# Handing out PSUM banks and softmax buffers by release, and a new order of the first part, in a recurrence and feed-forward kernel on one core

## The chip, the core and the metric

The kernel runs on one core of a Trainium2 chip. A core has five engines with queues of their own: TensorE (PE, matrix products, with its weight loads as PEld), VectorE (DVE), ScalarE (ACT), GpSimd (POOL) and SyncE (SP, which here starts nearly all DMAs). Matrix products land in PSUM, which has eight banks of 128 x 512 float32. The metric is the device time of one execution in microseconds (us), as the median of several runs; lower is better.

## The reference, cut to what matters

```python
batch, H, S, D, N, chunk = 4, 8, 768, 32, 16, 32
log_a = np.log(np.clip(a, 1e-06, 1.0))
for c in range(S // chunk):
    cum = np.cumsum(la, axis=-1)                        # la, xc, Bc, Cc: this chunk's
    L = np.exp(cum[:, :, :, None] - cum[:, :, None, :]) * causal
    M = np.einsum('bhin,bhjn->bhij', Cc, Bc) * L
    y_intra = np.einsum('bhij,bhjd->bhid', M, xc)
    y_inter = np.einsum('bhin,bhnd->bhid', Cc, state) * np.exp(cum)[:, :, :, None]
    y[:, :, sl] = y_intra + y_inter
    Bx = np.einsum('bhjn,bhjd->bhjnd', Bc, xc) * np.exp(cum[:, :, -1:] - cum)[..., None, None]
    state = np.exp(np.sum(la, axis=-1))[:, :, None, None] * state + np.sum(Bx, axis=2)
x = y as (3072 tokens, 256)
h = x @ w_in                                            # w_in: 256 x 2048
g = np.maximum(h, 0.0) + np.log1p(np.exp(-np.abs(h)))   # softplus
return g @ w_out                                        # w_out: 2048 x 256
```

## The kernel before

The 768 positions are cut into six rounds u of 128 positions. One round holds the four batches, 512 tokens in all, in two pairs of batches p. A round of the recurrence is made of these steps; the word in brackets is the one by which the order names it. Decay factors are exponentials of sums of logarithms, by token (`ft`) and by row (`fr`). POOL lays them out as a 128 x 512 triangle for each head pair (D, the affine selects that write `rm`). PE makes scores (S, four banks `sp` at a time, 32 short matmuls) and DVE multiplies them into the triangles (M, `rm<-sp,rm`). PE makes values within the round (I, `yp`), the new state (U, `zp`; N on DVE writes it as `tb`) and what the old state adds (R, also into `yp`, from C scaled by DVE, `cc`). DVE multiplies by the growth (G, `gg`). Then the result is split for the feed-forward part into a high part on ACT and a low part on DVE (Xh, Xl).

The feed-forward part of a round has 16 blocks k. Each is three products in split precision, high by high, low by high and high by low, of two halves of the contraction: six matmuls of 512 columns into a bank `hp` (F). ACT takes the softplus (`e<-hp`) and the high part `gh`, DVE the low part `gl<-e,gh` (P, in three stages). Six more matmuls add the block to the output sums in the two `acc` banks (Z): for each half of the output `gh` by the high weights, `gl` by the high weights, `gh` by the low weights `wol`, in this order. The weights themselves arrive as 64-bit numbers and are split on the way: three ACT steps, one DVE step that joins bits (`w<-w,signs`), the high part on ACT and the low part on DVE (`wil`, `wol`; the stages of W).

What sets the order. The whole first part is written out by hand as a string of words, `ORDER` (line 62); `act` looks each word up in the table `acts` and calls the step. Up to step 42 of the feed-forward part (`PINNED`) every instruction is kept in program order on its engine. Afterwards a scheduler orders the rounds 3 to 5, whose steps the table `FILLS` puts at given distances. All helpers record their operations in line 140, so rows of the profile carry L140 for most of the kernel, and are told apart by the names of the tiles.

What the change touches. `ps` (line 128) is a pool of six PSUM banks that are given out in rotation: the seventh tile takes the bank of the first, whoever has emptied its bank by then. Every `ps.tile` of log sums, factors, scores, `zp`, `yp` and `hp` comes from it. The softmax sums `e` rotate in the same way through three buffers of the pool `p3` (`parts_of`). `first_logs` (line 153) holds the logarithms of rounds 0 and 5 and a third group for the growth of round 0; `other_logs` holds the rest. `factors_by_token` makes fp (four products) and total (one), which PE works off in two passes each, and `factors_by_row` makes `sums` and `rp`; group 0 of each uses the first logs where it can. `warm` issues matmuls of 512 columns on a tile of zeros, `zeros<-some`, that nothing reads.

```python
ps = ctx.enter_context(tc.tile_pool(name="ps", bufs=6, space=PSUM))
pa = ctx.enter_context(tc.tile_pool(name="pa", bufs=1, space=PSUM))
e = p3.tile([P, 512], F32, tag="e", name=f"e{j}_{k}")
```

Of the kernel before, what the change touches and what calls it, by code (L numbers as in the profile page):

```python
# [41 lines left out]
ROW_GROUPS = ((1, LAST), (LAST, NU))  # L42
# [11 lines left out]
C_MID = C_OWN + (LAST - 1) * NB * (NC + 1)  # L54
# [6 lines left out]
la warm6 warm1 warm1 warm1 loga lb logb loga kb gc fr1 logr gb ft0 logr fr1 us0.0 ft0 ft0 w0 ft0 gc ft0 S0.0 growth  # L61
growth ft0 ux0.0 logb D0.0.0 D0.0.2 us0.1 M0.0.0 D0.0.1 M0.0.2 D0.0.3 W0 W0 M0.0.1 gq D0.1.0 ft1 ux0.1 M0.0.3 gq B0.0
W0 W0 fr0 I0.0 fr1 B0.1 gq gq ft1 D1.0.3 gq S0.1 G0.0 w2 Xh0.0 W2 W2 fr0 M0.1.0 W0 ft1 un1.0 W2 growth D0.1.1 M0.1.1
w1 fr0 D0.1.2 D0.1.3 fr0 M0.1.2 w4 ft1 fr1 D1.0.0 tl un1.1 M0.1.3 U0 W0 Xl0.0 I0.1 G0.1 Xh0.1 W2 W2 un2.0 N0 D1.1.0
S1.0 W4 Xl0.1 H0 W4 D1.0.2 M1.0.0 H1 W2 F0.1 M1.0.3 w6 W4 w3 P0.1 F0.0 D1.1.2 D1.1.3 T1 D1.0.1 F0.2 M1.0.2 D1.1.1 W4
P0.0 gd M1.0.1 W1 B1.1 S1.1 F0.3 W1 W4 M1.1.0 W1 W4 P0.2 w7 W1 w5 P0.0 M1.1.1 B1.0 W1 W1 F0.4 P0.0 P0.1 W6 P0.1 P0.2
M1.1.3 P0.3 P0.3 M1.1.2 W3 W3 W3 gg1 F0.5 Z0.0 C1 Z0.1 P0.2 W3 P0.4 W6 U1 N1 P0.3 I1.0 P0.5 W6 W6 W3 W3 I1.1 W6 D2.1.1
S2.0 P0.5 W7 R1 Z0.2 G1.0 D2.0.3 G1.1 Xh1.0 W7 P0.4 D2.0.2 D2.0.0 D2.0.1 W6 w10 Z0.3 M2.0.3 W7 F0.6 P0.6 Xh1.1 Xl1.0
W5 F0.7 Xl1.1 W7 P0.5 F1.5 M2.0.1 w12 W5 W7 W5 F1.0 P0.7 P0.7 P0.4 P0.6 W5 w14 P0.7 W5 W5 M2.0.0 F1.2 W12 M2.0.2 W12
D2.1.0 W12 F1.3 Z0.4 P1.3 B2.0 Z0.5 w9 P0.6 w8 W12 P1.0 W12 F1.6 W7 P1.2 W10 P1.3 W10 P1.3 P1.2 F1.1 P1.2 Z0.6 P1.1  # L70
Z0.7 K0.1 W10 P1.1 K0.0 W10 w11 P1.0 W12 P1.6 W10 P1.0 W10 F1.4 W9 F1.7 F0.12 P1.1 P1.4 Z1.0 P1.6 W9 P1.5 W8 W8 Z1.1
F1.12 W8 W8 un3.1 P1.6 Z1.2 D2.1.2 W9 P1.5 W8 F0.13 F1.10 P1.7 W9 W9 W8 Z1.3 F0.9 P1.5 W14 P0.12 W9 P1.4 P1.4 Z1.4
P0.9 W11 Z1.5 W14 W14 P0.12 W11 T2 W14 W11 W11 F0.8 Z1.6 w15 P1.7 P1.7 F0.10 P0.8 Z1.7 W11 gg3 P0.8 F0.11 W14 W11 W14
un3.0 P0.8 W15 K1.1 D2.1.3 F0.15 K1.0 w13 W13 Z0.8 W15 P0.10 P0.10 P0.9 F1.8 P0.12 P0.10 gg2 P0.13 P0.11 W13 W13 P0.9
W13 Z0.9 Z0.10 P0.15 P0.15 P0.11 P0.11 F0.14 P0.14 Z0.11 F1.11 P0.13 W13 un2.1 P0.14 P0.13 W13 P0.14 P0.15 Z0.12 Z0.13
W15 F1.9 W15 W15 P1.8 P1.8 P1.10 P1.11 W15 Z0.14 Z0.15 P1.8 D3.0.3 E0 P1.9 F1.14 Z1.8 B2.1 P1.9 P1.10 P1.9 C2 D3.0.2
P1.10 S2.1 M2.1.3 P1.12 M2.1.2 Z1.9 I2.0 P1.12 M2.1.0 M2.1.1 U2 I2.1 N2 P1.14 P1.14 P1.12 R2 P1.14 G2.0 S3.0 M3.0.2
D3.0.1 G2.1 P1.11 Xh2.0 Xl2.0 F1.15 Z1.10 M3.0.1 Xh2.1 P1.11 P1.15 P1.15 F1.13 D3.0.0 M3.0.3 Z1.11 P1.15 P1.13 M3.0.0
Xl2.1 P1.13 P1.13
"""  # L80
HALF = NFT // 2
# [14 lines left out]
    (-5, "U@ I@.0 I@.1 R@ S@+.0 G@.0 G@.1 N@ Xh@.0 Xh@.1 Xl@.0 Xl@.1"),  # L96
# [3 lines left out]
def constants():  # L100
# [7 lines left out]
    unit = np.arange((LAST - 1) * NB * (NC + 1)) // (NC + 1)  # L108
# [11 lines left out]
def recurrence_then_ffn(ctx: ExitStack, tc: tile.TileContext, un, alr, w_in, w_out, const, outT):  # L120
# [32 lines left out]
    first_logs = cp.tile([P, 3 * NR], F32, name="first_logs")  # L153
    other_logs = cp.tile([P, NA - 2 * NR + NL], F32, name="other_logs")
    lo, lr = other_logs[:, : NA - 2 * NR], other_logs[:, NA - 2 * NR :]
# [66 lines left out]
    def sum_logs():  # L222
        gp = ps.tile([P, 512], F32, tag="ps", name="log_sums")[:, :P]
        for b in range(NB):
            PE.matmul(
                gp[NR * b : NR * b + NR].rearrange("p (c k) -> p c k", k=SUB),
                first_logs[:, 2 * NR :],
                kc[:, : NC * (P + SUB)].rearrange("p (c k) -> p c k", k=P + SUB)[:, :, :SUB],
                start=True,
                stop=True,  # L230
            )
        yield
        by_head_row[0] = p3.tile([P, 2 * RT], F32, tag="xh", name="by_head_row")[:, :P]
        V.tensor_copy(by_head_row[0], gp)

    def growth_on_chip():
        gg_s[0] = p2.tile([P, 2, RT], F32, tag="gg", name="gg0")
        gp = [
            early_bank(b % 2, f"gp{b}") if b < 2 else ps.tile([P, 512], F32, tag="ps", name=f"gp{b}")
# [12 lines left out]
        for b in range(NB):  # L252
# [6 lines left out]
            )  # L259

# [32 lines left out]
    zeros = []  # L293

    def warm(n):
        if not zeros:
            zeros.append(ps.tile([P, 512], F32, tag="ps", name="zeros"))
        for _ in range(n):
# [6 lines left out]
            )  # L305

# [5 lines left out]
    cp.tile([P, 56], F32, name="apart")  # L312
    for u in range(NU):
        ks = slice(u * NR, (u + 1) * NR)
        f_tok[u] = ft[:, ks], fc[:, ks]
        f_row[u] = fr[:, u * NB : (u + 1) * NB]

    def factors_by_token(g):
        us = (0, LAST) if g == 0 else range(1, LAST)
        logs = first_logs[:, : 2 * NR] if g == 0 else lo  # L320
        n = len(us) * NR
        fp = ps.tile([P, 512], F32, tag="ps", name=f"fp{g}")
# [4 lines left out]
        runs = ((0, 1), (LAST, NU)) if g == 0 else ((1, LAST),)  # L327
        total, at = None, 0
        for u0, u1 in runs:
            here, cols = slice(at, at + (u1 - u0) * NR), slice(u0 * NR, u1 * NR)  # L330
            at = here.stop
            A.activation(fc[:, cols].rearrange("p k c -> p c k"), by_chunk[:, :, here], AF.Exp)
            yield
            if total is None:
                total = ps.tile([P, 512], F32, tag="ps", name=f"total{g}")[:, :n]
                PE.matmul(total, kc[:, NC * P : K_END], logs, start=True, stop=True)
                yield
            A.activation(ft[:, cols], total[:, here], AF.Exp)
            yield

    def factors_by_row(g):
        u0, u1 = ROW_GROUPS[g]
        logs = lo if g == 0 else first_logs[:, NR : 2 * NR]
        n, nu = (u1 - u0) * NR, (u1 - u0) * NB
        sums = ps.tile([P, 512], F32, tag="ps", name=f"sums{g}")[:n, : NC + 1]
        PE.matmul(sums, logs, kb[:, C_MID:C_HEAD], start=True, stop=True)
        yield
        by_head = p2.tile([P, (LAST - 1) * NB, NC + 1], F32, tag="by_head", name=f"by_head{g}", bufs=1)[:n, :nu]
# [5 lines left out]
        )  # L354
        yield
        rp = ps.tile([P, 512], F32, tag="ps", name=f"rp{g}")
# [95 lines left out]
    def update(u):  # L452
        zp = mid[u]["zp"] = ps.tile([P, 512], F32, tag="ps", name=f"zp{u}")
# [435 lines left out]
```

## Time and profile before

| what | before |
|---|---|
| median of 3 runs | 314.68 us (314.35 to 315.39) |
| profiled execution | 314.79 us, span 313.1 us |
| PE busy | 306.8 us, 98% of the span, 2325 matmul records |
| DVE busy | 155.8 us, 50% |
| ACT busy | 168.1 us, 54% |
| POOL busy | 43.6 us, 14% |
| DMA | 24.38 MB |

The times in this table and in the rows below are of one profiled execution, apart from the median. A row of the timeline is a run of like instructions on one engine: where it starts, how long it lasts, the operation with the tile written and the tiles read, shapes and count, and in brackets the idle time in front of it with what ended that. An instruction that has begun and is held up inside counts as busy, so starts of rows that follow one another are read along with the busy time.

### The profile page before, as it was taken

To read this page: it belongs to the slowest core of one execution; us is meant where nothing else is said; L and a number is where in the kernel's file an instruction comes from. 1 tells how busy PE (TensorE), PEld (TensorE's weight loads), DVE (VectorE), ACT (ScalarE), POOL (GpSimd) and SP (SyncE) were. 2 spreads that over 40 slices of the span, in tenths; PEclk is the share of its full clock that TensorE was granted. 3 is DMA by queue.
4 is the path that set the end of the run, shared out by engine and by line. 5 is a ranking of instruction groups with operands and counts; after the bars stand their busy time and mean duration, and the time that the engine had idled before them with its cause. 6 is when DMAs were issued, how large, how long until landed. Compare 5 with 4: busy or idle time off the path is not lost.

```text
span 313.1 us, 5688 instructions
## 1 busy us (share of the span) xinstructions
PE 306.8 (98%) x2325; PEld 251.8 (80%) x2325; DVE 155.8 (50%) x262; ACT 168.1 (54%) x292; POOL 43.6 (14%) x59
## 2 busy tenths in 40 slices
PE   8899999999999999999999999999999999999995
PEld 5778888888888788888888888888888888888884
DVE  5899866464566954453932352642352332322222
ACT  3898978778947244344344534344534344634450
POOL 2880710003130720100300000300000000000000
PEclk9999999999999999999999999999999999999999
DMA  7995442466201440100610100000100000100001
GB/s 214 404 386 163 137 134 69 167 176 214 81 0 67 137 137 4 66 0 0 228 45 0 67 2 0 4 0 0 67 4 0 2 0 2 67 0 0 2 0 67
DMA packets 10442, 24.38 MB, mean 78 GB/s; under 512 B 1200, under 2 KB 1840, under 8 KB 10416
## 3 DMA queue, kind: packets, MB, share of 16 engines
q1 hardware_dynamic: 10416, 24.02, 22.4%
q8 instruction: 18, 0.29, 0.4%
q14 instruction: 8, 0.07, 0.1%
HBM read 20.77 MB, written 3.24 MB: 77 GB/s over the span
## 4 chain that ended last, share of the span: by engine, by line
PE 95%; DVE 3%; ACT 1%; issue 0%; POOL 0%; POOLq 0%
PE acc L140 41%; PE hp L140 41%; PE yp L140 5%; PE sp L140 4%; DVE rm L140 1%; PE zeros L140 1%; PE end L140 1%; PE fp L140 1%; PE zp L140 1%; DVE xl L140 0%; DVE w L140 0%; DVE wil L140 0%; DVE gg L140 0%; ACT fc L140 0%; ACT signs L140 0%; PE rp L140 0%
## 5 line engine op out<-in xcount | busy, mean ns | idle before, releaser
L654 DVE TENSOR_TENSOR gl<-e,gh 128x512 fp32r<-128x512 f32 x54 | 37.3, 692 | 92.0 <-ACT gh L651 92.0
L140 PE MATMUL hp<-xh,wih 128*128 128x512 f32 (+1 forms) x196 | 75.8, 387 | 0.4 <-DVE gg L140 0.4
L140 PE MATMUL hp<-xh,wil 128*128 128x512 f32 (+1 forms) x196 | 75.4, 385 | 0.0
L140 PE MATMUL hp<-xl,wih 128*128 128x512 f32 (+1 forms) x196 | 75.4, 385 | 0.0
L140 PE MATMUL acc<-gh,woh 128*128 128x512 f32 x188 | 74.1, 394 | 0.0
L648 ACT ACTIVATE e<-hp 128x512 f32<-128x512 f32 x54 | 32.3, 598 | 77.7 <-PE hp L140 77.4
L140 PE MATMUL acc<-gl,woh 128*128 128x512 f32 x188 | 73.3, 390 | 0.0
L140 PE MATMUL acc<-gh,wol 128*128 128x512 f32 x188 | 73.2, 389 | 0.0
L140 PEld LDWEIGHTS hp<-xh,wih 128*128 128x128 f32 x196 | 36.8, 188 | 8.2 <-DVE gg L140 0.6
L140 DVE TENSOR_TENSOR gl<-e,gh 128x512 fp32r<-128x512 f32 x42 | 31.1, 749 | 24.3 <-ACT gh L140 24.2
L140 PEld LDWEIGHTS hp<-xl,wih 128*128 128x128 f32 x196 | 36.8, 188 | 7.3
L140 PEld LDWEIGHTS hp<-xh,wil 128*128 128x128 f32 x196 | 36.8, 188 | 7.3
L140 POOL TENSOR_SCALAR_AFFINE_SELECT rm<-fc 128x512 f32<-128x512 f32 x36 | 32.5, 939 | 70.2 <-ACT signs L140 41.9
L140 PEld LDWEIGHTS acc<-gh,woh 128*128 128x128 f32 x188 | 35.3, 188 | 8.2 <-ACT gh L140 0.2
L140 PEld LDWEIGHTS acc<-gh,wol 128*128 128x128 f32 x188 | 35.3, 188 | 7.4
L140 PEld LDWEIGHTS acc<-gl,woh 128*128 128x128 f32 x188 | 35.3, 188 | 7.3 <-DVE gl L654 0.2
L140 ACT ACTIVATE e<-hp 128x512 f32<-128x512 f32 x42 | 24.3, 592 | 23.8 <-PE hp L140 20.7
L651 ACT CAST gh<-e 128x512 fp32r<-128x512 f32 x54 | 33.5, 621 | 4.1 <-PE acc L140 2.4
L140 ACT CAST gh<-e 128x512 fp32r<-128x512 f32 x42 | 25.4, 616 | 5.3 <-PE acc L140 4.8
L140 ACT ACTIVATE signs<-wraw 128x512 f16<-128x512 f32 (+1 forms) x32 | 23.9, 781 | 0.0
L140 DVE TENSOR_TENSOR rm<-sp,rm 128x512 f32<-128x512 f32 x32 | 20.8, 682 | 3.7 <-PE sp L140 3.7
L404 POOL TENSOR_SCALAR_AFFINE_SELECT rm<-fc 128x512 f32<-128x512 f32 x12 | 9.1, 792 | 87.1 <-PE yp L140 69.4
(106 smaller groups left out, 212.3 us busy)
## 6 DMA issues: line engine op xcount, KB each, us to landing
un<-in_un SPq DMA_DIRECT2D x10, 768.0 KB, 6.4
wraw<-in_w_in SPq DMA_DIRECT2D x8, 512.0 KB, 5.0
wraw<-in_w_out SPq DMA_DIRECT2D x8, 512.0 KB, 3.8
gg<-gd SPq DMA_DIRECT2D x20, 128.0 KB, 3.9
out_t<-o SPq DMA_DIRECT2D x9, 256.0 KB, 2.1
head_in_h<-in_un SPq DMA_DIRECT2D x2, 384.0 KB, 5.2
head_in_l<-in_un SPq DMA_DIRECT2D x2, 384.0 KB, 6.9
out_t<-half SPq DMA_DIRECT2D x2, 256.0 KB, 2.1
```

What stands on the lines that cost most here:

```text
L140: return lambda *a, **k: tc.keep_in_program_order(f(*a, **k))
L404: Pl.affine_select(out=weights_of(u, p, ks.start, ks.stop).rearrange("p h (c i) -> p (h c) i", i=SUB), in_=fs.rearrange("p h c -> p (h c)" ...
L648: A.activation(e, h, AF.Softplus)
L651: A.copy(gh, e)
L654: V.tensor_tensor(gl, e, gh.bitcast(F32), op=ALU.subtract)
```

## The change

Four edits go together. The six banks become six tiles of one buffer each, and a list of free banks is kept while the program is written: `take` hands out the bank that came back first, and `done` is called right after the last step that reads it, so the next tile takes the bank which is emptied first in the order of the program. The three softmax buffers are handled in the same way. The first logs hold rounds 0, 1, 2 and 5 instead of 0 and 5 (160 columns instead of 96; the other logs 256 instead of 320 ahead of the growth), and the columns of all factors follow this order of rounds. `ORDER` is a new string, in which the nine warm matmuls are six, one, one and one. In `FILLS` one word, N, stands earlier in its row.

```diff
-ROW_GROUPS = ((1, LAST), (LAST, NU))
+SLOTS = (0, 1, 2, LAST, 3, 4)
+NS = 4
...
 ORDER = """
-la warm6 warm1 warm1 warm1 loga lb logb loga kb gc fr1 logr gb ft0 logr fr1 us0.0 ft0 ft0 w0 ft0 gc ft0 S0.0 growth
...
+warm6 la loga loga lb logr logr growth ft0 logb ft0 kb ft0 warm1 us0.0 gc ft0 growth D0.0.0 ft0 ft0 D0.1.3 D0.0.1 gb
...
-    (-5, "U@ I@.0 I@.1 R@ S@+.0 G@.0 G@.1 N@ Xh@.0 Xh@.1 Xl@.0 Xl@.1"),
+    (-5, "U@ I@.0 I@.1 R@ N@ S@+.0 G@.0 G@.1 Xh@.0 Xh@.1 Xl@.0 Xl@.1"),
...
-    ps = ctx.enter_context(tc.tile_pool(name="ps", bufs=6, space=PSUM))
+    ps = ctx.enter_context(tc.tile_pool(name="ps", bufs=1, space=PSUM))
...
+    class Ring:
+        def __init__(self, pool, tag, n, dtype):
+            self.pool, self.tag, self.dtype = pool, tag, dtype
+            self.free, self.held = deque(range(n)), {}
+        def take(self, name):
+            k = self.held[name] = self.free.popleft()
+            return self.pool.tile([P, 512], self.dtype, tag=f"{self.tag}{k}", name=name, bufs=1)
+        def done(self, name):
+            self.free.append(self.held.pop(name))
+    banks = Ring(ps, "ps", 6, F32)
+    soft = Ring(p3, "e", 3, F32)
...
-    first_logs = cp.tile([P, 3 * NR], F32, name="first_logs")
-    other_logs = cp.tile([P, NA - 2 * NR + NL], F32, name="other_logs")
+    first_logs = cp.tile([P, (NS + 1) * NR], F32, name="first_logs")
+    other_logs = cp.tile([P, NA - NS * NR + NL], F32, name="other_logs")
...
-            mid[u]["sp", p, q] = ps.tile([P, 512], F32, tag="ps", name=f"sp{u}_{p}{q}")
+            mid[u]["sp", p, q] = banks.take(f"sp{u}_{p}{q}")
...
         V.tensor_tensor(m, mid[u].pop(("sp", p, q)), m, op=ALU.mult)
+        banks.done(f"sp{u}_{p}{q}")
...
-        e = p3.tile([P, 512], F32, tag="e", name=f"e{j}_{k}")
+        e = soft.take(f"e{j}_{k}")
         A.activation(e, h, AF.Softplus)
+        banks.done(f"hp{j}_{k}")
...
         V.tensor_tensor(gl, e, gh.bitcast(F32), op=ALU.subtract)
+        soft.done(f"e{j}_{k}")
```

The order on the engines at three places. The first is PE in the opening, behind the leading warm matmuls (`zeros`); `fp` and `total` are the sums for the factors by token, `sums` those by row, `sp_00` the first score of round 0. Before:

```order
L140 MATMUL zeros<-some 32x512
L140 MATMUL log_sums<-kc,first_logs 32x128 x4
L140 MATMUL sums_130<-kb,first_logs 32x5
L140 MATMUL fp_135<-first_logs,kc 128x64 x4
L140 MATMUL total_145<-first_logs,kc 128x64
L140 MATMUL sp_00_153<-head_in_h 128x128
```

And with the change:

```order
L159 MATMUL zeros<-some 32x512
L159 MATMUL fp_123<-first_logs,kc 128x128 x4
L159 MATMUL total_131<-first_logs,kc 128x128
L159 LDWEIGHTS some
L159 MATMUL zeros<-some 32x512
L159 MATMUL log_sums<-kc,first_logs 32x128 x4
L159 MATMUL sp_00_155<-head_in_h 128x128
```

The sums of the factors have moved ahead of the log sums and are twice as wide, a warm matmul stands behind them, and `sums` has left this place.

The second is PE at the scores of the second pair of round 1 (`sp_10` to `sp_13`), behind the last matmul of block 2 of the feed-forward part, with the semaphores that each waits for. Before:

```order
L140 MATMUL hp_2_415<-xh_270,wil 128x512
L140 MATMUL sp_10_433<-un_282 128x128 [waits DMAHW4_49,DVE_49]
L140 MATMUL sp_11_434<-un_282 128x128 [waits DVE_49]
L140 MATMUL sp_12_435<-un_282 128x128 [waits DVE_49]
L140 MATMUL sp_13_436<-un_282 128x128 [waits Activation_49]
```

And with the change:

```order
L159 MATMUL hp_2_423<-xh_269,wil 128x512
L159 MATMUL sp_10_430<-un_305 128x128 [waits DMAHW4_49,DVE_49]
L159 MATMUL sp_11_431<-un_305 128x128 [waits DVE_49]
L159 MATMUL sp_12_432<-un_305 128x128 [waits Activation_49]
L159 MATMUL sp_13_433<-un_305 128x128 [waits Activation_49]
```

The block stands behind the same matmul; the third of its banks is now one that ACT empties.

The third is DVE around the state products of round 1 (`tb`), up to the low part of the output weights for the first output sums (`wol_85`). Before:

```order
L140 TENSOR_TENSOR cc_526<-un_282,fr 128x256 x2
L140 TENSOR_TENSOR gl_2_535<-e_2_465,gh_2_494 128x512
L140 SCALAR_TENSOR_TENSOR w_502<-w_502,signs_81 128x512
L140 SCALAR_TENSOR_TENSOR tb_558<-zp_541,kb,td_412 128x4x32 x2
L140 TENSOR_TENSOR gl_3_561<-e_3_497,gh_3_499 128x512
L140 SCALAR_TENSOR_TENSOR w_490<-w_490,signs_80 128x512
L140 TENSOR_TENSOR wol_85<-w_502,woh_84 128x512
L140 TENSOR_TENSOR gg_506<-yp_0_563,gg_506 128x512
```

And with the change:

```order
L159 SCALAR_TENSOR_TENSOR w_465<-w_465,signs_80 128x512
L159 SCALAR_TENSOR_TENSOR tb_545<-zp_516,kb,td_493 128x4x32 x2
L159 TENSOR_TENSOR cc_548<-un_305,fr 128x256 x2
L159 TENSOR_TENSOR gl_2_555<-e_2_490,gh_2_533 128x512
L159 TENSOR_TENSOR gl_3_557<-e_3_535,gh_3_541 128x512
L159 SCALAR_TENSOR_TENSOR w_538<-w_538,signs_81 128x512
L159 TENSOR_TENSOR wol_85<-w_465,woh_84 128x512
L159 TENSOR_TENSOR gg_585<-yp_0_565,gg_585 128x512
```

The scalings of C and the low part of block 2 have moved from ahead of the state products to behind them, and one w from behind to ahead; `wol` stays the last of the group.

## Rows read from the trace of the kernel before

**Rows 1.** The page, busy time of each engine over the span.

```profile
PE 306.8 (98%) x2325; PEld 251.8 (80%) x2325; DVE 155.8 (50%) x262; ACT 168.1 (54%) x292; POOL 43.6 (14%) x59
```

**Rows 2.** Chain that ended last: its shares by engine; a piece (start us, us, what).

```profile
PE 95%; DVE 3%; ACT 1%; issue 0%; POOL 0%; POOLq 0%
...
47.16 2.72 PE acc L140 x12
```

**Rows 3.** PE's waits from 0 to 110 us: us in total, times, longest.

```profile
PE zeros L140 <- POOL level L140: 1.0, 1, 1.0
PE rp L140 <- DVE rm L140: 0.4, 1, 0.4
```

**Rows 4.** PE's timeline in the opening: start us, us, what, count, [idle before].

```profile
0.98 3.59 PE L140 MATMUL zeros<-some 128*32 128x512 bf16 x8 [0.98 <-POOL level L140]
...
4.24 0.43 PE L140 MATMUL log_sums<-kc,first_logs 128*32 128x128 f32 x3
...
5.41 1.64 PE L140 MATMUL fp<-first_logs,kc 128*128 128x64 f32 x8
...
7.21 1.17 PE L140 MATMUL sp<-head_in_h 32*128 32x128 f32 x32
...
9.26 1.13 PE L140 MATMUL fp<-other_logs,kc 128*128 128x128 f32 x8 [0.43 <-ACT signs L140]
```

**Rows 5.** The timeline of ACT, POOL and DVE in the opening.

```profile
3.89 0.28 ACT L140 ACTIVATE first_logs<-first_logs 128x96 f32<-128x96 f32 x1 [1.81 <-DVE first_logs L140]
...
7.56 3.45 POOL L140 TENSOR_SCALAR_AFFINE_SELECT rm<-fc 128x512 f32<-128x512 f32 x5 [4.94 <-ACT ft L140]
...
8.47 2.58 DVE L140 TENSOR_TENSOR rm<-sp,rm 128x512 f32<-128x512 f32 x4 [1.69 <-PE sp L140]
```

**Rows 6.** PE's timeline at the second scores of round 1.

```profile
22.45 0.49 PE L140 MATMUL sp<-un 32*128 32x128 f32 x4
...
23.36 1.16 PE L140 MATMUL sp<-un 32*128 32x128 f32 x28 [0.42 <-DVE rm L140]
```

**Rows 7.** PE's timeline from the state matmuls of round 1 to the output sums.

```profile
31.47 0.65 PE L140 MATMUL zp<-un,bp 128*32 128x64 f32 x32
...
33.80 1.17 PE L140 MATMUL sp<-un 32*128 32x128 f32 x32
...
35.94 0.50 PE L140 MATMUL acc<-gh,woh 128*128 128x512 f32 x1
```

**Rows 8.** DVE's timeline in the same stretch.

```profile
30.10 0.75 DVE L140 TENSOR_TENSOR cc<-un,fr 128x256 f32<-128x256 f32 x2
...
32.27 0.60 DVE L140 SCALAR_TENSOR_TENSOR tb<-zp,kb,td 128x128 f32<-128x128 f32 x2
...
32.79 0.68 DVE L140 TENSOR_TENSOR gl<-e,gh 128x512 fp32r<-128x512 f32 x1
...
33.90 0.69 DVE L140 SCALAR_TENSOR_TENSOR w<-w,signs 128x512 int32<-128x512 int32 x1 [0.43 <-ACT signs L140]
...
34.51 1.19 DVE L140 TENSOR_TENSOR wol<-w,woh 128x512 fp32r<-128x512 f32 x1
```

**Rows 9.** POOL's timeline in the same stretch.

```profile
33.10 7.54 POOL L140 TENSOR_SCALAR_AFFINE_SELECT rm<-fc 128x512 f32<-128x512 f32 x8 [9.81 <-PE yp L140]
```

**Rows 10.** The timeline of DVE without, then of POOL and DVE with, selects.

```profile
89.14 0.69 DVE L140 TENSOR_TENSOR gl<-e,gh 128x512 fp32r<-128x512 f32 x1 [1.82 <-ACT gh L140]
...
104.05 7.30 POOL L140 TENSOR_SCALAR_AFFINE_SELECT rm<-fc 128x512 f32<-128x512 f32 x8 [11.31 <-issue]
...
104.94 2.16 DVE L140 TENSOR_TENSOR gl<-e,gh 128x512 fp32r<-128x512 f32 x2
```

**Rows 11.** PE's timeline at the first scores behind the first part.

```profile
106.18 1.17 PE L140 MATMUL sp<-un 32*128 32x128 f32 x32
...
107.75 0.50 PE L140 MATMUL hp<-xh,wih 128*128 128x512 f32 x1 [0.40 <-DVE gg L140]
```

**Rows 12.** Windows, 0 to 7 us: length, busy by engine (count), PEclk, DMA share, GB/s.

```profile
0.00:7.00 7.00, 6.02 (x28) 3.57 (x29) 4.46 (x16) 1.93 (x3) 1.90 (x11) 1.00 0.67 196
```

More of the change, by code (lines that the diff above doesn't have):

```diff
@@ L1 @@
-from collections import defaultdict
+from collections import defaultdict, deque
 from contextlib import ExitStack
@@ L66 @@
[L66 to L70, printed above, removed]
@@ L80 @@
+P1.9 D3.0.2 M3.0.3 P1.14 F1.13 M3.0.1 M3.0.0 P1.15 Xh2.0 Z1.9 Z1.10 P1.13 Z1.11 P1.12 Xl2.1 P1.12 Xl2.0 P1.13 P1.13
+M3.0.2 P1.14 P1.14
 """
+WARM = sum(int(w[4:]) for w in ORDER.split() if w.startswith("warm"))
 HALF = NFT // 2
@@ L234, in sum_logs @@
         V.tensor_copy(by_head_row[0], gp)
+        banks.done("log_sums")
     def growth_on_chip():
@@ L259, in growth_on_chip @@
             )
+            if b > 1:
+                banks.done(f"gp{b}")
     def load_growth(u):
@@ L305, in warm @@
             )
+        spent[0] += n
+        if spent[0] == WARM:
+            banks.done("zeros")
     f_tok, f_row = {}, {}
@@ L311, in recurrence_then_ffn @@
     fr = cp.tile([P, NU * NB, NC + 1], F32, name="fr")
-    cp.tile([P, 56], F32, name="apart")
-    for u in range(NU):
-        ks = slice(u * NR, (u + 1) * NR)
+    cp.tile([P, 72], F32, name="apart")
+    for at, u in enumerate(SLOTS):
+        ks = slice(at * NR, (at + 1) * NR)
         f_tok[u] = ft[:, ks], fc[:, ks]
-        f_row[u] = fr[:, u * NB : (u + 1) * NB]
+        f_row[u] = fr[:, at * NB : (at + 1) * NB]
     def factors_by_token(g):
[L319 to L322, printed above, removed]
+        logs = first_logs[:, : NS * NR] if g == 0 else lo
+        n = logs.shape[1]
+        fp = banks.take(f"fp{g}")
         for i in range(NC):
@@ L326, in factors_by_token @@
         by_chunk = fp[:, : NC * n].rearrange("p (c k) -> p c k", c=NC)
[L327 to L332, printed above, removed]
+        total = None
+        for a, b in ((0, NR), (NR, n)) if g == 0 else ((0, n),):
+            cols = slice(g * NS * NR + a, g * NS * NR + b)
+            A.activation(fc[:, cols].rearrange("p k c -> p c k"), by_chunk[:, :, a:b], AF.Exp)
+            if b == n:
+                banks.done(f"fp{g}")
             yield
             if total is None:
-                total = ps.tile([P, 512], F32, tag="ps", name=f"total{g}")[:, :n]
+                total = banks.take(f"total{g}")[:, :n]
                 PE.matmul(total, kc[:, NC * P : K_END], logs, start=True, stop=True)
                 yield
-            A.activation(ft[:, cols], total[:, here], AF.Exp)
+            A.activation(ft[:, cols], total[:, a:b], AF.Exp)
+            if b == n:
+                banks.done(f"total{g}")
             yield
     def factors_by_row(g):
[L342 to L345, printed above, removed]
+        logs = lo if g else first_logs[:, NR : NS * NR]
+        n = logs.shape[1]
+        nu = n // NH
+        at = NS * NB if g else NB
+        sums = banks.take(f"sums{g}")[:n, : NC + 1]
         PE.matmul(sums, logs, kb[:, C_MID:C_HEAD], start=True, stop=True)
         yield
-        by_head = p2.tile([P, (LAST - 1) * NB, NC + 1], F32, tag="by_head", name=f"by_head{g}", bufs=1)[:n, :nu]
+        by_head = p2.tile([P, (NS - 1) * NB, NC + 1], F32, tag="by_head", name=f"by_head{g}", bufs=1)[:n, :nu]
         V.tensor_tensor(
@@ L354, in factors_by_row @@
         )
+        banks.done(f"sums{g}")
         yield
-        rp = ps.tile([P, 512], F32, tag="ps", name=f"rp{g}")
+        rp = banks.take(f"rp{g}")
         PE.matmul(
@@ L489, in next_state @@
             )
+            banks.done(f"zp{u}")
             return
@@ L499, in next_state @@
             )
+        banks.done(f"zp{u}")
     def values_of(u):
@@ L678, in second @@
             for c in range(0, 512, 256):
-                end = ps.tile([P, 512], F32, tag="ps", name=f"end{c}")
+                end = banks.take(f"end{c}")
                 for v in range(NFT - END, NFT):
```

64 lines of the change are left out of this document (35 added, 29 removed).

## The prediction, made before the changed kernel had run

> **What bounds the kernel now.** I read the page's shares first, then the chain that ended last, then TensorE's waits, and only then single stretches. TensorE (PE) is busy for 306.8 us, 98% of the span of 313.1 [rows 1], and the chain runs through it for 95% of the span [rows 2]. Of the rest, 1.0 lies ahead of its first matmul [rows 3]. Once the feed-forward products run, twelve of 512 columns take 2.72 us, 0.227 each, and nothing waits [rows 2]. So no change of order can make the steady part shorter: the count of matmuls is the same, and what can change is the time in which PE stands. Behind that first one, no wait that the trace names up to 110 us is over 0.4 [rows 3], but a matmul that waits can be booked as busy, so starts have to be compared as well. There are three such places: the opening up to 18 us, the scores at 22.45 us, and the stretch from 105 to 108 us. The other engines are half idle; they matter where PE needs the last of what they do.
>
> The profiled execution took 314.79 us, 1.7 around its span of 313.1; the median of the runs is 314.68, so I make the sum against 314.79 and take 0.1 off.
>
> **Opening (first logs, warm matmuls, new order).** Before, nine warm matmuls reach from 0.98 to the first sums at 4.24 [rows 4]. Now six stand there. At 0.41 each (eight take from 0.98 to 4.24) they end near 3.5, and PE idles until the logarithms are there. These are 160 columns wide instead of 96, which I price at 0.1 more on the path through VectorE (DVE) and ScalarE (ACT), from the 0.28 that 96 columns took on ACT [rows 5]: PE goes on near 4.4. The factor sums come first now, eight passes and then two. Before, those ten took 1.80 us, from 5.41 to the scores at 7.21 [rows 4], so they end near 6.3 to 6.5 instead of 7.21, and GpSimd (POOL) can begin its selects some 0.8 earlier than 7.56 [rows 5]. But what those selects are for, the four DVE products that end at 11.0, begins at 8.47 when the scores are done [rows 5]. Behind the sums PE still has a warm matmul, the log sums and the 1.17 us of scores [rows 4], so the scores again begin near 7.2 and the 0.8 is lost there. Two of the three moved warm matmuls (0.227 each now) stand ahead of waits for DVE and cost nothing; one I count. Behind it the same DVE work releases the same PE work in much the same succession. Value taken: **+0.2**; bounds -0.4 (half of the 0.8 gets through) and +0.5 (none does, and all three warm matmuls are paid).
>
> **Banks by release.** Before, the second scores of round 1 start four matmuls at 22.45 and go on at 23.36, after 0.42 of visible idleness that a DVE product ended; the block takes 2.07 us (to 23.36 and 1.16), and the same 32 records take 1.17 at 33.80 [rows 6, 7]. The bank that came next by rotation was the one that DVE emptied last. Now the list hands out the bank that program order empties first, and in the new order the third score waits for ACT instead of DVE. **-0.9**; bounds -0.9 and 0 (DVE has the same products to do, and a later matmul may wait for them).
>
> **The weights of the first output sums.** This is the term on which the sum turns. From the state matmuls of round 1 (zp) to the output sums (acc) PE has the same work in both versions, only with scores and values swapped: 31.47 to 35.94, 4.47 us [rows 7]. The third matmul, which needs the low part of the output weights (wol), comes two of 512 columns later, 0.45 by their 0.227, or about 5.0 us after zp begins. What DVE does in that time is not the same. Before: two state products, one gl, w and wol, and wol ends at 35.70 (34.51 and 1.19), 4.2 after zp: in time [rows 8]. Now: two state products, two scalings of C (0.75 us for both), gl, gl, w, wol. If each of the last four took the 0.69 that a gl takes alone [rows 10], wol would end 0.80 (from zp to the state products) + 0.52 (these, to gl) + 0.75 (the scalings) + 4 x 0.69, or 4.83 us after zp: in time again [rows 7, 8]. But POOL works off eight selects from 33.10, 1.6 after zp [rows 9], and has the same eight now. Beside selects two gl in a row took 2.16 us instead of 1.38, and eight selects 7.30 us instead of some 0.7 each as in the opening (five in 3.45) [rows 5, 10]: DVE instructions with two inputs in SBUF and the selects go in turns. A turn is then about 1.1 us. With all four paying, wol ends 2.07 + 3 x 1.1 + 1.2 = 6.6 us after zp, and the acc matmuls stand 1.6 us. **+1.6**; bounds 0 (no turn is paid) and +1.8. I take the upper part because POOL's eight last 7.5 us, longer than the four DVE instructions, and no DVE instruction that reads PSUM stands between them to let POOL get ahead.
>
> **Later.** The block at 106.18 takes 1.57 to the next hp instead of some 1.1, since that hp waited for a bank that DVE empties late [rows 11]; with the list a score waits there instead, for a bank that ACT empties once a softmax buffer is free, and that buffer hangs on one gl beside selects (+0.4 of a turn over 0.69): -0.5 and +0.25, **-0.25** in all; bounds -0.5 and +0.3. The selects that fill round 3 ahead of time are now four close together with w, cc and gl ahead of the first part's last output sums. A turn costs 0.4 over 0.69 [rows 10], and I let half of one through: **+0.2**, bounds 0 and +0.5. The softmax ring itself has three buffers as before and its release follows the same gl: 0, hidden while ACT is about half idle [rows 1], and paid only where gl is late, which the two terms hold. The planner's table for the last rounds gains one moved word (N), and the PE order from round 3 on is the same blocks: 0, with 0.2 either way.
>
> Sum: 0.2 - 0.9 + 1.6 - 0.25 + 0.2 = **+0.85**: 315.64, less 0.1, **315.5 us**.
>
> **Rivals.**
> The turns are not paid (38%). If at most one of the four meets a select, because POOL starts later or DVE earlier than I place them, wol is in time, and the term is 0: 0.2 - 0.9 - 0.25 = -0.95, **313.7 us**. The point of decision is wol's end 5.0 us after zp begins. For it: before, w at 33.90 took 0.69 beside a select, unslowed, and wol alone paid [rows 8]. Against it: that w came after a wait of 0.43, when a select had just ended; the pair at 104.94 came without pauses and paid on both [rows 10], and so do these four.
>
> PE's clock rises later (17%). In the trace 512 columns take 0.41 us at the start and 0.227 later, and eight passes of 64 columns 1.64 where eight of 128 take 1.13 from 9.26 [rows 2, 4]: the step from 1.2 to 2.4 GHz falls between 5.4 and 7.2, and up to there the matmuls followed one another without a gap. The window's granted clock reads 1.00 throughout and does not show it [rows 12]. With PE standing from 3.5 to 4.4 the rise may fall behind the scores. Scores and two warm matmuls then take twice their time, 1.17 + 0.45, and the log sums their 0.43 again instead of half: some 1.8 us more, of which about 0.6 lies in waits that follow. That is +1.2 on top, **316.7 us**. The Trainium skill (TensorE: Matmul & The Clock Gate, The HAM clock gate) has the half rate as the resting state, which activity releases, and says that the moment varies between runs; by it the shorter warm-up speaks against the change, and the time would be this rival's. The trace agrees with two rates and one rise, and cannot show what a gap does, so one in six.
>
> The rings change nothing (3%): the third score still waits for DVE, 0.9 is not gained, 316.4 us.
>
> **How the numbers follow.** My forecast has 42%, with 315.0 to 316.0 of its own from its smaller terms. A measurement tells 0.3%, 0.94 us, from no change: faster is below 313.74, slower above 315.62. Of the forecast's 42%, 18 lie above and none below; the first rival lies on the lower bound, and of its 38 I put 21 below, as its later terms may gain up to their bounds, and 17 within; the second and third, 20, lie above. Together 21% faster, 41% the same, 38% slower. The range takes in both outer rivals and leaves out what lies beyond the bounds of their terms: 313.3 to 316.7.
>
> **What would show it.** In the changed trace: the second scores of round 1 should be one block of about 1.2 us. The first acc block should start 0.4 to 1.1 us earlier than before, since 0.9 is gained by then. Behind yp and scores near 35 us PE should stand 1 to 1.6 us for DVE's wol, with gl, gl, w and wol at 1.1 us between starts beside selects. If PE stands less than 0.3 there, the first rival is right. If the scores of round 0 take over 2 us instead of 1.17, the clock has risen late. A first acc block no earlier than before with none of these says that the opening was lost by something that I have not priced, and a PE wait over 0.5 us beyond 120 us that the planner's part was not neutral.

## The result and the profile after

The changed kernel took 316.91 us in the median of 15 runs (315.32 to 318.23), the kernel before 314.69 (314.23 to 316.39). The ratio is 1.0061, with a 95% interval of 1.0046 to 1.0076: slower by 0.61%, or 1.9 us. The forecast of 315.5 was too low. By the ratio the time is 316.6, at the upper end of the range of 313.3 to 316.7; the median itself lies 0.2 above that range. The outcome, slower, had 38%. The runs of the changed kernel are spread over 2.9 us, those of the kernel before over 2.2: five of the fifteen lie from 315.3 to 316.1 and ten from 316.9 to 318.2, with none between.

The profiled execution took 317.45 us with a span of 315.7, 2.6 more than before. First the page, busy time of each engine, and two of TensorE's waits over the whole span (us in total, times, longest):

```profile
PE 309.4 (98%) x2325; PEld 253.1 (80%) x2325; DVE 156.9 (50%) x262; ACT 169.3 (54%) x292; POOL 45.4 (14%) x59
```

```profile
PE acc L159 <- DVE wol L159: 0.9, 1, 0.9
PE fp L159 <- ACT first_logs L159: 0.6, 1, 0.6
```

The busy time rose by 2.6 us with the same 2,325 matmul records [rows 1]: most of the loss is booked as busy. The named waits hold 0.9 us for wol, a new one, and 0.6 us ahead of the factor sums. So the starts have to be compared. TensorE's timeline in the opening, after (start us, us, what, count, [idle before]):

```profile
0.97 2.74 PE L159 MATMUL zeros<-some 128*32 128x512 bf16 x6 [0.97 <-POOL level L159]
4.34 2.08 PE L159 MATMUL fp<-first_logs,kc 128*128 128x128 f32 x8 [0.62 <-ACT first_logs L159]
...
6.78 0.61 PE L159 MATMUL zeros<-some 128*32 128x512 bf16 x1
...
7.74 2.30 PE L159 MATMUL sp<-head_in_h 32*128 32x128 f32 x32
9.97 0.53 PE L159 MATMUL zeros<-some 128*32 128x512 bf16 x1
...
11.56 0.39 PE L159 MATMUL zeros<-some 128*32 128x512 bf16 x1
...
19.80 0.39 PE L159 MATMUL hp<-xh,wih 128*128 128x256 f32 x1
...
24.25 1.17 PE L159 MATMUL sp<-un 32*128 32x128 f32 x32
...
29.56 0.39 PE L159 MATMUL acc<-gh,woh 128*128 128x512 f32 x1
```

The single warm matmuls are a gauge of the clock: the same 512 columns take 0.61 us at 6.78, 0.53 at 9.97 and 0.39 at 11.56. So the step from 1.2 to 2.4 GHz came near 10 us. The scores of round 0 took 2.30 us; before, they took 1.17 [rows 4]. The second scores of round 1, at 24.25, are one block of 1.17 us; before, they were two with a stall between [rows 6]. Three starts of the timeline before, to compare with: the first hp, the first output sums, and the first hp behind the output sums of blocks 2 and 3, which after stands at 41.28 (last row of the next block). That hp is block 6 of round 0 before and block 7 of round 0 after; one of the expectations below calls it the first hp of round 1.

```profile
17.79 0.38 PE L140 MATMUL hp<-xh,wih 128*128 128x256 f32 x1
...
28.66 0.39 PE L140 MATMUL acc<-gh,woh 128*128 128x512 f32 x1
...
38.81 0.39 PE L140 MATMUL hp<-xh,wih 128*128 128x512 f32 x1
```

And the stretch from the state matmuls of round 1 on, after, on TensorE, VectorE and GpSimd:

```profile
32.37 0.65 PE L159 MATMUL zp<-un,bp 128*32 128x64 f32 x32
...
35.73 1.59 PE L159 MATMUL sp<-un 32*128 32x128 f32 x32
37.25 0.50 PE L159 MATMUL acc<-gh,woh 128*128 128x512 f32 x1
...
38.87 0.50 PE L159 MATMUL acc<-gh,wol 128*128 128x512 f32 x1 [0.89 <-DVE wol L159]
...
41.28 0.39 PE L159 MATMUL hp<-xh,wih 128*128 128x512 f32 x1
```

```profile
34.29 2.31 DVE L159 TENSOR_TENSOR gl<-e,gh 128x512 fp32r<-128x512 f32 x2
36.52 1.19 DVE L159 SCALAR_TENSOR_TENSOR w<-w,signs 128x512 int32<-128x512 int32 x1
37.63 1.19 DVE L159 TENSOR_TENSOR wol<-w,woh 128x512 fp32r<-128x512 f32 x1
```

```profile
34.00 7.80 POOL L159 TENSOR_SCALAR_AFFINE_SELECT rm<-fc 128x512 f32<-128x512 f32 x7 [9.83 <-PE yp L159]
```

The four DVE instructions gl, gl, w and wol take 1.1 to 1.2 us each while the selects run, and wol ends at 38.82, 6.45 us after zp begins; the third acc matmul starts right behind it. The block of scores ahead took 1.59 us instead of 1.17.

From these starts the 2.6 us come apart: up to the first hp 19.80 - 17.79 = +2.0; from there to the first output sums (29.56 - 19.80) - (28.66 - 17.79) = -1.1; from there to the hp behind the output sums of blocks 2 and 3 (41.28 - 29.56) - (38.81 - 28.66) = +1.6; and all the rest of the kernel +0.1. In that rest a piece of twelve matmuls takes 2.72 us as before [rows 2]:

```profile
48.47 2.72 PE acc L159 x12
```

### The profile page after: what moved, and what is told of

Its sections match the earlier page's. It is cut to its first block, busy times and chain, and to the rows that moved or that the text cites. A ratio compares the mean times of both kernels' runs of the same rounds, so it can differ in the third digit from the quotient of the medians.

```text
span 315.7 us, 5677 instructions
## 1 busy us (share of the span) xinstructions
PE 309.4 (98%) x2325; PEld 253.1 (80%) x2325; DVE 156.9 (50%) x262; ACT 169.3 (54%) x292; POOL 45.4 (14%) x59
## 4 chain that ended last, share of the span: by engine, by line
PE 95%; DVE 3%; issue 1%; ACT 0%; DVEq 0%
PE hp L159 42%; PE acc L159 41%; PE sp L159 4%; PE yp L159 4%; PE fp L159 1%; PE zp L159 1%; PE end L159 1%; DVE kc L159 1%; DVE rm L159 1%; DVE gl L159 0%; DVE wol L159 0%; DVE cc L159 0%; ACT fc L159 0%; DVE tb L159 0%; PE log_sums L159 0%
## 5 line engine op out<-in xcount | busy, mean ns | idle before, releaser
L159 POOL TENSOR_SCALAR_AFFINE_SELECT rm<-fc 128x512 f32<-128x512 f32 x36 | 34.4, 991 | 72.8 <-ACT signs L159 39.1
L433 POOL TENSOR_SCALAR_AFFINE_SELECT rm<-fc 128x512 f32<-128x512 f32 x12 | 9.1, 790 | 85.3 <-PE yp L159 69.4
```

What stands on the lines that cost most here:

```text
L159: return lambda *a, **k: tc.keep_in_program_order(f(*a, **k))
L433: Pl.affine_select(out=weights_of(u, p, ks.start, ks.stop).rearrange("p h (c i) -> p (h c) i", i=SUB), in_=fs.rearrange("p h c -> p (h c)" ...
```

## The experiments

Eleven kernels ran. Each time is a median beside runs of the kernel before on the same chip. The chips differ between experiments, so the ratio to before decides, with its 95% interval, and differences between two versions are taken from their ratios. The theory was that three parts hold the change: the clock in the opening (a loss), the banks (a gain), the turns of VectorE with the selects (a loss).

| run | median us | ratio to before | interval |
|---|---|---|---|
| e1, before + rings, tiles shifted | 315.96 | 1.0041 | 1.0027 to 1.0054 |
| e2, changed + 8 warm | 315.64 | 1.0029 | 1.0018 to 1.0040 |
| e3, before, 6 warm | 315.64 | 1.0031 | 1.0020 to 1.0043 |
| e4, changed + select gate, tiles shifted | 322.05 | 1.0231 | 1.0217 to 1.0244 |
| e5, before + rings | 313.90 | 0.9977 | 0.9963 to 0.9991 |
| e6, changed + select gate | 314.65 | 0.9990 | 0.9972 to 1.0007 |
| e7, changed + gate + 8 warm | 313.88 | 0.9971 | 0.9957 to 0.9986 |
| e8, before, tiles shifted | 322.29 | 1.0236 | 1.0205 to 1.0267 |
| e9, before + rings + logs | 313.71 | 0.9971 | 0.9959 to 0.9983 |
| e10, e7 without single warms | 314.58 | 0.9990 | 0.9979 to 1.0000 |
| e11, e2 + wol earlier | 316.93 | 1.0069 | 1.0054 to 1.0085 |

**e2: eight warm matmuls at the front of the changed kernel.**

```diff
-warm6 la loga loga lb logr logr growth
+warm8 la loga loga lb logr logr growth
```

> The changed kernel with eight warm matmuls at the front instead of six, which fill the time in which TensorE stands before the factor sums (3.5 to 4.34 us); the three later ones stay. Theory (the standing in the opening lets the clock rise late, at about 10 us instead of between 5.4 and 7.2): the clock rises before the scores of round 0, these take about 1.2 us instead of 2.30, the first hp starts 1.2 to 1.6 us earlier than 19.80, and the time is 1.2 to 1.6 us under that of the changed kernel, some 315.2 us. Rival (the opening is late by its order and the wider logs): the two added matmuls change nothing, within 0.3 us of the changed kernel (316.6 to 316.9).

The ratio fell from 1.0061 to 1.0029, about 1.0 us, somewhat less than expected, and the runs drew together (315.33 to 316.33). TensorE's timeline of e2:

```profile
4.50 1.23 PE L159 MATMUL fp<-first_logs,kc 128*128 128x128 f32 x8
...
5.88 0.39 PE L159 MATMUL zeros<-some 128*32 128x512 bf16 x1
...
6.82 1.39 PE L159 MATMUL sp<-head_in_h 32*128 32x128 f32 x32 [0.34 <-DMA head_in_h<-in_un]
...
17.93 0.38 PE L159 MATMUL hp<-xh,wih 128*128 128x256 f32 x1
...
37.00 0.50 PE L159 MATMUL acc<-gh,wol 128*128 128x512 f32 x1 [0.89 <-DVE wol L159]
```

The gauge reads 0.39 already at 5.88, the scores take 1.39, and the first hp stands at 17.93, 1.87 us earlier than in the changed kernel and 0.14 later than before. The wait for wol is the same 0.89. So the loss in the opening goes with the two matmuls, and the wait for wol does not depend on it.

**e3: six warm matmuls in the kernel before.** The three words `warm1` are taken out of its order.

```diff
-la warm6 warm1 warm1 warm1 loga lb logb loga
+la warm6 loga lb logb loga
```

> The kernel before with its three single warm matmuls taken out, six left, nothing else changed: TensorE stands from about 3.5 to 4.24 us. Theory (late clock): the scores of round 0 take over 2 us instead of 1.17 and the time is 1.0 to 1.5 us above before, near 316.0. Rival (the clock rises when it does without regard to these three): the log sums go on 0 to 0.2 us earlier, and the time is that of before or 0.2 under it.

315.64 us, ratio 1.0031: slower by 1.0 us, as the theory had it in size, but not by the sign that it named. In the profiled execution the scores of round 0 took 1.17 us: the clock had risen early. Two other things went wrong in this execution. First, ScalarE stood 2.27 us for raw weights that a DMA delivered by 9.12, its gg came late, and TensorE stood 1.22 us for that; the sums at 14.20 began 1.0 us later than before (13.19 there):

```profile
6.27 1.17 PE L139 MATMUL sp<-head_in_h 32*128 32x128 f32 x32
...
10.79 1.08 PE L139 MATMUL yp<-rm,head_in_h 128*32 128x128 f32 x32 [1.22 <-ACT gg L139]
...
14.20 0.49 PE L139 MATMUL total<-other_logs,kc 128*128 128x128 f32 x2
```

```profile
9.12 0.68 ACT L139 ACTIVATE w<-wraw 128x512 f32<-128x512 f32 x1 [2.27 <-DMA wraw<-in_w_in]
```

Second, the clock fell again later. The windows of e3 (from:to, length, busy by engine (count), PEclk, DMA share, GB/s):

```profile
8.00:12.00 4.00, 2.46 (x45) 2.23 (x45) 3.03 (x6) 2.88 (x7) 1.89 (x3) 1.00 1.05 407
12.00:15.00 3.00, 2.38 (x37) 1.88 (x36) 2.06 (x6) 2.95 (x6) 2.08 (x4) 1.00 1.01 390
15.00:19.00 4.00, 4.00 (x88) 3.33 (x91) 3.49 (x7) 2.97 (x7) 1.95 (x3) 0.57 1.02 412
```

Here the granted clock shows in the profile: a mean of 0.57 from 15 to 19 us, between the two levels, after a stretch from 8 to 15 us in which TensorE had been busy for 4.84 of 7 us. Why it fell in this run and not in the others with long waits there is open. The first hp stood at 19.43, 1.64 us later than before, so the fall accounts for some 0.6 of that. Neither event explains the median. A mean granted clock of 0.995, which such a fall gives, shows in only two of the nine runs, the others have 0.999 or 1.000; and e1, with nine warm matmuls in front, got its raw weights as late (9.14). So what six matmuls cost in the kernel before stays open, and e3 does not show that it is a late clock.

**e4 and e6: holding back the selects.** One select of a single column, which reads a column of wol, stands ahead of round 2's selects on GpSimd, so that the selects start when wol is written. Nothing else moves. In e4 its result had a tile of its own, in e6 it goes to a spare column of an existing tile (e6's edit):

```diff
-    level = cp.tile([P, 9], F32, name="level")[:, :1]
+    levels = cp.tile([P, 9], F32, name="level")
+    level = levels[:, :1]
...
+    def gate():
+        Pl.affine_select(
+            out=levels[:, 8:],
+            in_=wo["l", 0][:, 2, :1].bitcast(F32),
+            pattern=[[1, 1]],
+            compare_op=ALU.is_ge,
...
-I1.0 D2.1.3 gg1
+I1.0 gate D2.1.3 gg1
```

> The changed kernel with one tiny select on GpSimd (one column, which nothing reads) put ahead of the eight selects of round 2; it reads a column of wol, so that the eight start only when DVE has written wol. The order of all other engines is as it was. Theory (gl, gl, w and wol go in turns with the selects): these four DVE instructions take about 0.7 us each, the wait of 0.9 us for wol is gone, the block of scores ahead of it is not held up either, and the time is 1.2 to 1.6 us under the changed kernel, near 315.2. Rival (DVE has too much to do there in any case, and the selects cost nothing): the wait stays at 0.7 us or more, and round 2 may start its products later, so the time is that of the changed kernel (316.6) or up to 1 us above.

e4 took 322.05 us and neither theory had that. Its wait for wol was gone, but all matmuls of the feed-forward part had become slower: a piece of twelve in the chain that ended last takes 2.80 us instead of 2.72 [rows 2].

```profile
46.51 2.80 PE acc L159 x12
```

The tile of its own had moved the tiles allocated behind it by 32 bytes. So e6 repeated it with every tile where it lies in the changed kernel.

> The changed kernel with the tiny select ahead of round 2's selects, now writing to a spare column of the tile that holds level, so that every tile lies where it lies in the changed kernel; with a tile of its own it had moved the later tiles by 32 bytes, and the pitch of the matmuls rose from 227 to 234 ns. Theory (turns with the selects): pitch 227, no wait for wol, first hp of round 1 (41.28 in the changed kernel) about 1.4 us earlier against the opening, time 1.2 to 1.6 us under the changed kernel, 315.1 to 315.5. Rival (DVE is late there anyway): pitch 227 and a time within 0.4 us of the changed kernel.

314.65 us, ratio 0.9990: 2.2 us under the changed kernel, more than expected. TensorE, VectorE and GpSimd in the same stretch of e6:

```profile
30.51 0.65 PE L159 MATMUL zp<-un,bp 128*32 128x64 f32 x32
...
33.87 1.17 PE L159 MATMUL sp<-un 32*128 32x128 f32 x32
34.97 0.50 PE L159 MATMUL acc<-gh,woh 128*128 128x512 f32 x1
...
37.85 0.39 PE L159 MATMUL hp<-xh,wih 128*128 128x512 f32 x1
```

```profile
32.42 1.28 DVE L159 TENSOR_TENSOR gl<-e,gh 128x512 fp32r<-128x512 f32 x2
33.63 0.68 DVE L159 SCALAR_TENSOR_TENSOR w<-w,signs 128x512 int32<-128x512 int32 x1
34.28 0.69 DVE L159 TENSOR_TENSOR wol<-w,woh 128x512 fp32r<-128x512 f32 x1
```

```profile
35.04 0.19 POOL L159 TENSOR_SCALAR_AFFINE_SELECT level<-wol 128x1 f32<-128x1 f32 x1 [12.85 <-DVE wol L159]
35.18 7.14 POOL L159 TENSOR_SCALAR_AFFINE_SELECT rm<-fc 128x512 f32<-128x512 f32 x7
```

The same instructions in the same order take 1.28, 0.68 and 0.69 us, wol ends 4.46 us after zp begins, and neither the scores nor acc wait: from zp to the hp behind the output sums 7.34 us instead of 8.91, 1.57 less, and as long as in the kernel before (38.81 - 31.47). This shows the turns. What the time gained beyond that is to be sought in the opening: this execution's clock had risen early with the same six warm matmuls, as two rows show.

```profile
4.34 1.16 PE L159 MATMUL fp<-first_logs,kc 128*128 128x128 f32 x8 [0.63 <-ACT first_logs L159]
...
5.66 0.39 PE L159 MATMUL zeros<-some 128*32 128x512 bf16 x1
```

How often that happened in the runs without a profile isn't seen; they spread from 313.23 to 315.66.

**e1 and e5: the rings alone.** The order of before, its two groups in the first logs and its factors by row, with the rings, and N ahead in the table, without which the list runs out of banks. The unused tile `apart`, which nothing reads, has 56 columns in the kernel before and 72 in the changed one. e1 kept the 72, e5 has the 56. Against the changed kernel (cut; the last two lines are e5's alone):

```diff
-SLOTS = (0, 1, 2, LAST, 3, 4)
-NS = 4
+SLOTS = (0, LAST, 1, 2, 3, 4)
+NS = 2
...
-    cp.tile([P, 72], F32, name="apart")
+    cp.tile([P, 56], F32, name="apart")
```

> The kernel before with the banks and softmax sums handed out by release, its own order and its own first logs (rounds 0 and 5), and N moved ahead in the table of the last rounds, which the list of six banks needs. Theory (the rings alone gain the stall at the second scores of round 1): that block is one of about 1.2 us instead of 2.07, the first output sums start 0.9 us earlier (near 27.75 instead of 28.66), nothing else moves, and the time is 0.7 to 0.9 us under before. Rival (the score waits for DVE whichever bank it gets): within 0.2 us of before.

315.96 us, 1.3 us above before, against the theory. But the profile had the second scores of round 1 in one block, and matmul pieces that were too long:

```profile
47.15 2.75 PE acc L159 x12
```

> The kernel before with rings (banks and softmax sums by release, N moved ahead in the table), this time with the unused tile apart at 56 columns as before, so that every tile lies where it lay before; the run before this one had 72 there, and its matmuls of 512 columns followed one another at 229 ns instead of 227 from 120 us on. Theory (the rings gain the stall at the second scores of round 1, the address cost the rest): the pitch is 227 ns again, the second scores of round 1 are one block of about 1.2 us, and the time is 0.6 to 0.9 us under before. Rival (the rings cost something later in the kernel): the pitch stays at 229 ns and the time about 1 us above before.

313.90 us, ratio 0.9977, 0.7 us under before. The piece takes 2.72 again, and the scores are one block:

```profile
45.89 2.72 PE acc L159 x12
```

```profile
17.39 0.39 PE L159 MATMUL hp<-xh,wih 128*128 128x256 f32 x1
...
22.05 1.17 PE L159 MATMUL sp<-un 32*128 32x128 f32 x32
...
27.36 0.39 PE L159 MATMUL acc<-gh,woh 128*128 128x512 f32 x1
```

From the first hp to the first output sums e5 needs 9.97 us and the kernel before 10.87: the rings give 0.90 there. From the first output sums to the end of the span both need 284.4 us.

**e8: the address alone.** The unused tile of the kernel before is made eight columns wider, 32 bytes.

```diff
-    cp.tile([P, 56], F32, name="apart")
+    cp.tile([P, 64], F32, name="apart")
```

> The kernel before with the unused tile apart 64 columns wide instead of 56, and nothing else: the tiles of the splits and of the feed-forward data lie 32 bytes further, the weights where they were. Theory (the address of the moving data sets the pitch): 234 ns between matmuls of 512 columns instead of 227, and with about 1,700 of them up to 6 us more time after the opening, 319 to 322 us. Rival (the longer pitch came from the select or from the rings): 227 ns and the time of before.

322.29 us in two runs, ratio 1.0236, just above the expected 319 to 322. The sum in the expectation was off: six rounds of 16 blocks with twelve such matmuls are 1,152 and not 1,700, and 96 pieces of twelve at 0.08 us more each are 7.7 us; the two spans differ by 7.0. Nothing else is changed, and the piece of twelve takes 2.80:

```profile
47.62 2.80 PE acc L140 x12
```

That accounts for e4 and for most of e1: in e1 the tiles behind the unused one lay 64 bytes further against the weights than in before (2.75, 229 ns each), in e4 and e8 32 bytes (2.80, 233 ns). From the first output sums to the end e1's profiled execution needs 286.6 us where e5's needs 284.4, 2.2 more, and the medians differ by 2.1. Whether the distance from the weights counts or the place of the data by itself was not separated.

**e7, e10: both repairs.** e7 joins the diffs of e2 and e6.

> The changed kernel with both: eight warm matmuls at the front, and the tiny select that holds round 2's selects until wol is written. Theory (the two losses are separate and add up): 1.2 (as measured for the warm matmuls alone) and 1.2 to 1.6 under the changed kernel, 313.8 to 314.3, which is 0.5 to 1.0 under before. Rival (a gain in one place is given back at the next wait): 315.2 or more.

313.88 us, ratio 0.9971: 0.9 us faster than before, as expected. Its profiled execution, which took 314.94 us, 1.1 over the median, has a wait that e6's does not have, 0.5 us at 89.43 for a gl of DVE, so in that one a part was given back there. e10 also leaves out the three single warm matmuls.

```diff
-ft0 kb ft0 warm1 us0.0
+ft0 kb ft0 us0.0
...
-ux0.0 warm1 D0.1.0
+ux0.0 D0.1.0
...
-B0.0 warm1 us0.1
+B0.0 us0.1
```

> The changed kernel with eight warm matmuls at the front, the tiny select ahead of round 2's selects, and without the three single warm matmuls that stand between the log sums, the scores and the values. Theory (these stand in the way of gp and yp by 0.1 to 0.3 us each, and the clock has risen by then): 0.2 to 0.5 us under the version with them (313.88), 313.4 to 313.7. Rival (they keep the clock up): without them the clock falls back in some runs, the runs scatter by over 1.5 us, and the median is 314.3 or more.

314.58 us, ratio 0.9990: a miss. Without the three the kernel is 0.6 us slower, not faster. The runs scatter by 1.67 us, as the rival said, but in the profiled execution the clock did not fall; TensorE waited for DVE's rm products in yp instead, 0.4 us in all. Yet the first hp stands at 17.85, earlier than the 18.22 of e7's, so the opening of this execution does not show the loss. The cause stays open.

**e9: rings and first logs on the order of before.** The changed kernel with `ORDER` put back to that of before, but for the two words for the factors by row; `SLOTS`, `NS` and the unused tile are the changed kernel's.

> The kernel before with rings and with the first logs of four rounds, on the order of before (the two words for the factors by row change places, since the first logs now hold rounds 1 and 2), with the addresses of the changed kernel. Theory (the wider first logs are neutral: the passes over them have the same count and ACT's work moves from the second group to the first): within 0.3 us of rings alone, 313.6 to 314.2. Rival (160 columns instead of 96 hold up the start): 0.4 to 0.8 us over rings alone, 314.3 to 314.7.

313.71 us, ratio 0.9971, beside e5's 0.9977 with overlapping intervals: the wider first logs are neutral. This is also the lowest median of all, though not told apart from e7 and e5. Since e9 differs from the changed kernel in `ORDER` alone, it splits the result: by the ratios (1.0061 and 0.9971) the new order costs 2.8 us, and the other three edits together gain 0.9. Of the 2.8, e2 gives back 1.0 and e6's select 1.57 in the trace, and e7 with both has the ratio of e9.

**e11: wol one place earlier on DVE, with eight warm matmuls.**

```diff
-w7 P0.2 P0.3 P0.5 W3 W6 W6 W3 I1.0
+w7 P0.2 P0.3 P0.5 W3 W3 W6 W6 I1.0
```

> The changed kernel with eight warm matmuls at the front and with wol one place earlier on DVE, ahead of the joining of bits (w) that stood before it; the selects are left alone. Theory (gl, gl, w and wol go in turns with the selects, so that their place does not matter as long as the selects run): the wait for wol shrinks from 0.9 to under 0.3 us, and what is gained comes back as a wait or a slow start at the first products of round 1 (hp, waiting for xl or xh), so the time is within 0.3 us of that with eight warm matmuls alone (315.64), 315.4 to 315.9. Rival (wol only stood too late in the order): the wait goes and is not paid again, 314.6 to 314.9.

The wait for wol is gone, and the time is not better but worse, 316.93 us. TensorE's waits of e11:

```profile
PE hp L159 <- ACT xh L159: 0.8, 1, 0.8
PE hp L159 <- DVE xl L159: 0.2, 1, 0.2
```

The wait has moved to the first products of round 1, as the theory said, since DVE still goes in turns with the selects and reaches gg and xl no earlier: counted from zp the first gg starts 6.37 us later in both e2 and e11, and the first xl, behind a wil that now takes 1.11 us beside a select, 0.6 later than in e2. That the median is 1.3 us above e2, where the theory had 0.3, isn't explained: in the profiles 0.9 us lie between the two by the first products of round 1, half of them in the opening.

## Why the prediction was right or wrong, step by step

**Opening, +0.2 (-0.4 to +0.5): the step that failed.** The term priced the moved work, let the clock rise as before, and left a later rise to a rival. Measured was +2.0 in the profiled execution, where the clock rose near 10 us. The seven profiled executions of the new order part by the clock: in the five where it had risen by 6.6 us the first hp stands at 17.85 to 18.37 (17.93 in e2, 17.92 in e6), in the two where it rose later at 19.27 (e4) and 19.80. Against the 17.79 of before the early ones are +0.1 to +0.6. So the price of the moved work was right as far as single executions tell (in the old order with an early clock the first hp ranges from 17.39 in e5 to 18.61 in e1), and what came was the rival "PE's clock rises later". I had it at 17% and +1.2; it cost 1.9 in the profiled execution (19.80 - 17.93) and 1.0 by the ratios of e2. In that execution the 1.8 that I counted for the slower matmuls came whole; the 0.6 of it that I let vanish in waits did not vanish. That its 316.7 is 0.1 from the measured 316.6 is luck in part, since 1.2 lies between these two. The reason that I gave, TensorE standing from 3.5 to 4.4, is borne out by e2 in its effect: filling that gap took away 1.0 us. But it does not force a late rise. With six leading warm matmuls the profiled executions show one rise near 10 us (changed), one before 9.53 (e4, where the gauge reads 0.61 at 6.78), and two by 6 (e6 with 0.39 at 5.66, e3 with eight factor sums in 1.10 at 4.84); with eight or nine it came by 7.2 us in all nine. So in these executions six leading matmuls left the moment open over some 4 us, and eight or nine did not. Four executions against nine are few, and no run without a profile shows its clock in the opening. The two groups in the times of the changed kernel would fit two moments, with five runs about where e2's lie; but e3 and e4, with six as well, spread over 1.2 and 0.1 us only. The Trainium skill (TensorE: Matmul & The Clock Gate, Part 1: The HAM clock gate) says that the moment varies between runs of the same kernel; these traces agree, before 6 and near 10 us for the same opening (e6 and the changed kernel), which is far more than the half microsecond either way that the section gives for sustained work; here the warm-up has a pause in it, and the measurement counts.

**Banks, -0.9: right.** -0.90 between the first hp and the first output sums in e5, where the rings stand without the new order, and -0.7 in its time. The changed kernel's -1.1 in that stretch holds 0.2 more, which belongs to the new order. The rival that they change nothing is out.

**The weights of the first output sums, +1.6: right, size and mechanism.** Measured +1.6; wol ended 6.45 us after zp where I had 6.6, and the four turns were 1.1 to 1.2 us where I had 1.1. e6 takes the selects away and with them the loss of 1.57. Not all of it is the wait that I named: 0.4 us lay in the scores ahead, which took 1.59 instead of 1.17 and in e6 take 1.17 again. The rival "the turns are not paid" is out. The Trainium skill (SBUF — State Buffer, SBUF: two separate sides) calls the port pair that VectorE and GpSimd share an exclusive lock, held for a whole instruction, which a VectorE operation with two inputs in SBUF contends for with a GpSimd operation that reads SBUF; the rows agree, with gl at 0.64 without and 1.16 beside selects.

**Later, -0.25 and +0.2: right in sum.** +0.1 behind 41.28. The scores behind the first part took 1.59 us and the next hp came at once, so there the wait only changed its place, and nothing was seen of the second term.

**First logs, softmax ring, N: 0, right** as far as e9 and e5 show it.

The sum failed by the clock alone: 0.85 was forecast, 0.7 is what the profiled execution's +2.6 leaves when 1.9 of it goes to the clock, and e2, with the clock up early, has the ratio 1.0029, or 315.6 where the forecast was 315.5. The chances had the forecast and the turn rival far ahead of the clock, which was wrong: the gap from 3.5 to 4.4 stood in the forecast itself and deserved more than one in six.

## What to carry to other kernels

Count the matmuls at the start as part of the schedule: two fewer at the front (six instead of e2's eight) cost 1.0 us here although TensorE had nothing else to do at the time. A VectorE chain that feeds TensorE should not meet GpSimd's selects; holding GpSimd back by one tiny dependent instruction gave back 1.6 us, where a better place for the late instruction only moved the wait. Compare the pitch of the steady matmuls before anything else when an experiment adds a tile.

## What the runs showed of the hardware that was not expected

The place of the data in SBUF changes the pitch of the fp32r matmuls: with the tiles of the data moved by 32 bytes against the weights a piece of twelve took 2.80 us instead of 2.72, and the whole kernel 7.4 us more by the ratio (e8, two runs); moved by 64 bytes 2.75 (e1). And the clock can fall again after it has risen: the mean of 0.57 from 15 to 19 us in e3.
